# A second gated layer whose output is accumulated transposed in five of six token groups, with right-side tiles shifted by 96 bytes

## The chip, the cores and the metric

The kernel runs on one core of one Trainium2 chip. The metric is device time in microseconds (us) of the whole launch. An execution can be profiled: the profile has a start, an end and operands for the instructions of TensorE (PE, and PEld for its weight loads), VectorE (DVE), ScalarE (ACT), GpSimd (POOL) and SyncE (SP, which here only issues DMAs and waits).

## The reference, cut to what matters

A delta-rule attention over 4 batches of 768 tokens (8 heads of 48) gives rows of 384 numbers. Two dense layers follow, on 3,072 rows:

```python
h = np.maximum(x @ w_in, 0.0)            # 384 -> 2048
x = (h * h @ w_out)                      # 2048 -> 384
gate = 1.0 / (1.0 + np.exp(-(x @ w_gate)))   # 384 -> 1536
val = x @ w_val                              # 384 -> 1536
out = (gate * val @ w_out)                   # 1536 -> 384
```

The change lies in the last line, the product of `gate * val` (called p here) with the second `w_out`, 1536 by 384.

## The kernel before, in words

Tokens are cut into six groups of 512 (two chunks of 64 tokens of each of the four batches). In the first stage attention and the first layer run interleaved in an order written out by hand. The second stage (`moe2_h`, `moe2_o`, and the loop at L848) is the second layer alone, and the change is in it.

Every float32 operand is cut into a high and a low part of the type float32r, and each product is made in three passes: high by high, high by low, low by high. For each group g the layer's 1,536 inner features are cut into 12 blocks f of 128, so the stage has 72 steps n = 12g + f.

`moe2_h(n)` (L792) makes the gate and the val of one block: for each of the two, 3 passes by 3 blocks of 128 inputs, 9 matmuls at L802 with 512 moving columns (the tokens) and 128 by 128 stationary weights. Then ACT takes the sigmoid (L808), DVE multiplies (p, L810), ACT makes the high part `ph` (L812) and DVE the low part `pl` (L814).

`moe2_o(n)` (L819) adds the block's share to the output. Its stationary operand is `ph` or `pl` for one of four blocks m of 128 tokens, its moving operand the 384 columns of `w_out`: 12 matmuls at L832 a step, and each PSUM tile holds 128 tokens by 384 outputs. Three of its four PSUM tiles (o0 to o2) have a bank each, the fourth has one from another pool. After block 11 each tile is copied to SBUF by ACT (m = 0, 2; L841) or DVE (m = 1, 3; L839), and two DMAs each write 64 rows of 1,536 bytes (L845), eight a group.

The loop at L848 issues `moe2_h(n)` and then `moe2_o(n - 1)`, so TensorE always has a step of L802 between two steps of L832, and the last block's `moe2_o` of a group comes just after the first `moe2_h` of the next. At f = 2 SP loads the next group's input (L753, tile x2r); at f = 6, 7, 8 ACT and POOL split a third of it each (L758, helper lines L115 and L116). Each engine works through its own instructions in program order, and so does SP.

The weights of blocks f = 0 to 5 (`w2a`, L764) lie on the right side of SBUF, under the pool `w2x` (L763: staging for weights and input, and the sigmoid's tile). Those of f = 6 to 11 (`w2b`, L786) lie on the left, as do the tiles of x, `ph` and `pl`. A block's tile has 384 columns each of gate, val and output weights, once for the high part and once for the low.

Of the kernel before, what the change touches and what calls it, by code (L numbers as in the profile page):

```python
# [7 lines left out]
F32 = mybir.dt.float32  # L8
# [7 lines left out]
NB, NH, SEQ, HD = 4, 8, 768, 48  # L16
DM, FF1, FF2 = 384, 2048, 1536
C = 64
NSTEP = SEQ // C
NG = NSTEP // 2  # L20
# [63 lines left out]
def kernel(  # L84
# [637 lines left out]
    with tc.manual_schedule():  # L722
        for token in ORDER.split():
            run(token)
        w2_t, w2_new = {}, []

        def open_w2(fs, name, side):
            pool = ctx.enter_context(tc.tile_pool(name=name, bufs=1, side=side, reuse_waits="tile"))
            for f in fs:
                w2_t[f] = [pool.tile([128, 3 * DM], F32R, name=f"w2{h}{f}") for h in ("h", "l")]  # L730
                w2_new.append(f)

        w2_in = []

        def w2_load():
            if w2_new:
                f = w2_new.pop(0)
                t = w2x.tile([128, 3 * DM], F32, tag="t", name="t")
                nc.sync.dma_start(out=t, in_=w2d[:, f * 3 * DM:(f + 1) * 3 * DM])
                w2_in.append((f, t))  # L740

        def w2_split(n=1):
            while len(w2_in) > n:
                f, t = w2_in.pop(0)
                split(*w2_t[f], t, nc.vector)

        x2 = {}

        x2r = {}

        def load_x2(g):
            x2r[g] = w2x.tile([128, KD, GT], F32, tag="x2r", name="x2r")
            nc.sync.dma_start(out=x2r[g], in_=x2d[g])  # L753

        def split_x2(g, kc):
            if kc == 0:
                x2[g] = [work.tile([128, KD, GT], F32R, tag=f"x{h}", name=f"x{h}") for h in ("hi", "lo")]
            split(x2[g][0][:, kc], x2[g][1][:, kc], x2r[g][:, kc], nc.gpsimd)  # L758

        N1 = NG * NF1  # L760
        assert not (kt_t or kc_t or kn_t or v_t or q_t or pm_t or N_t or xr_t or yt_t or o_t)
        at.close()
        w2x = ctx.enter_context(tc.tile_pool(name="w2x", bufs=2, side="right"))  # L763
        open_w2(range(W2A), "w2a", "right")  # L764
        for n in range(N1 - NF1 + 2, N1 + 2):
            if n < N1:
                moe1_h(n)
            if n + 2 < N1:
                fetch_low(n + 2, 0)
            if n + 1 < N1:  # L770
                fetch_low(n + 1, 1)
            if n < N1:
                w2_split()
            moe1_o(n - 2)
            if n == N1 + 1:
                put_x2(NG - 1)
            if n < N1:
                if n % 2:
                    w2_load()
                moe1_g(n)  # L780
            if n == N1 - 7:
                load_x2(0)
            if N1 - 5 <= n < N1 - 2:
                split_x2(0, n - N1 + 5)
        p1.close()
        open_w2(range(W2A, NF2), "w2b", "left")  # L786

        obp = ctx.enter_context(tc.tile_pool(name="obp", bufs=4))
        ps_2 = ctx.enter_context(tc.tile_pool(name="ps_2", bufs=4, space=PSUM))
        p_t = {}  # L790

        def moe2_h(n):  # L792
            g, f = divmod(n, NF2)
            assert f not in w2_new and all(f != i for i, _ in w2_in)
            xh, xl = x2[g]
            pss = []
            for v in range(2):
                hi, lo = (w[:, v * DM:(v + 1) * DM] for w in w2_t[f])
                ps = ps_2.tile([128, GT], F32, tag="gv", name="gv")
                for i, (w, x) in enumerate([(hi, xh), (lo, xh), (hi, xl)]):  # L800
                    for kc in range(KD):
                        nc.tensor.matmul(  # L802
                            out=ps, lhsT=w[:, kc * 128:kc * 128 + 128], rhs=x[:, kc, :],
                            start=(i == 0 and kc == 0), stop=(i == 2 and kc == KD - 1),
                        )
                pss.append(ps)
            sg = w2x.tile([128, GT], F32, tag="sg", name="sg")
            nc.scalar.activation(out=sg, in_=pss[0], func=ACTF.Sigmoid)  # L808
            p = work.tile([128, GT], F32, tag="gg", name="p")
            nc.vector.tensor_tensor(out=p, in0=sg, in1=pss[1], op=ALU.mult)  # L810
            ph = work.tile([128, GT], F32R, tag="gh", name="ph", bufs=3)
            nc.scalar.copy(out=ph, in_=p)  # L812
            pl = work.tile([128, GT], F32R, tag="gl", name="pl", bufs=3)
            nc.vector.tensor_tensor(out=pl, in0=p, in1=ph.bitcast(F32), op=ALU.subtract)  # L814
            p_t[n] = (ph, pl)

        po2 = [None] * 4

        def moe2_o(n):  # L819
            g, f = divmod(n, NF2)  # L820
            if f == 0:
                po2[:] = [
                    ps_o.tile([128, DM], F32, tag=f"o{m}", name=f"o{m}") if m < 3
                    else ps_2.tile([128, DM], F32, tag="o3", name="o3", bufs=1)
                    for m in range(4)
                ]
            hi, lo = (w[:, 2 * DM:3 * DM] for w in w2_t[f])
            ph, pl = p_t.pop(n)
            for m in range(4):
                cs = slice(m * 128, m * 128 + 128)  # L830
                for i, (x, w) in enumerate([(ph, hi), (ph, lo), (pl, hi)]):
                    nc.tensor.matmul(  # L832
                        out=po2[m], lhsT=x[:, cs], rhs=w,
                        start=(f == 0 and i == 0), stop=(f == NF2 - 1 and i == 2),
                    )
                if f == NF2 - 1:
                    ob = obp.tile([128, DM], F32, tag="ob", name="ob")
                    if m % 2:
                        nc.vector.tensor_copy(out=ob, in_=po2[m])  # L839
                    else:  # L840
                        nc.scalar.copy(out=ob, in_=po2[m])  # L841
                    s = 2 * g + m // 2
                    for b in range(2):
                        r0 = (2 * (m % 2) + b) * SEQ + s * C
                        nc.sync.dma_start(out=out[r0:r0 + C, :], in_=ob[64 * b:64 * b + 64])  # L845

        N2 = NG * NF2
        for n in range(N2 + 1):  # L848
            if n < N2:
                moe2_h(n)  # L850
                w2_split(n < 2)
                g, f = divmod(n, NF2)
                if f == 2 and g + 1 < NG:
                    load_x2(g + 1)
                if 6 <= f < 9 and g + 1 < NG:
                    split_x2(g + 1, f - 6)
            w2_load()
            if n >= 1:
                moe2_o(n - 1)
# [5 lines left out]
def _layout(inputs):  # L865
    import numpy as np

    q, k, v, beta = (np.asarray(inputs[n]) for n in ("q", "k", "v", "beta"))

    def cut(a):  # L870
        return a.reshape((2, 2, 4, 2, NSTEP, C) + a.shape[3:])


    def places(x):
        x = cut(x)
        return np.stack([np.stack([x[:, a ^ c, :, a] for c in range(2)]) for a in range(2)])


    qc, kc, vc, bc = places(q), places(k), places(v), places(beta)

    def dims(x):
        return x.transpose(0, 6, 4, 1, 2, 3, 5).reshape(96, NSTEP, 16, C)

    def by_c(x):
        return x.transpose(1, 5, 4, 0, 2, 3, *range(6, x.ndim)).reshape((128, NSTEP, 16) + x.shape[6:])

    def by_a(x):
        return x.transpose(0, 5, 4, 1, 2, 3, 6).reshape(128, NSTEP, 16, HD)

    def lhs(w):  # L890
        return w.reshape(KD, 128, -1, 128).transpose(1, 2, 0, 3).reshape(128, -1, DM)

    def rhs(w):
        return w.reshape(-1, 128, DM).transpose(1, 0, 2)

    i = {n: np.ascontiguousarray(a).view(np.int64) for n, a in inputs.items() if n.startswith("moe")}
    arrays = {
        "kq": np.stack([dims(kc), dims(qc)], axis=2),
        "kn": by_c(kc),
        "vn": by_c(vc),  # L900
        "ks": by_a(kc),
        "beta": by_c(bc),
        "w1": np.concatenate([lhs(i["moe_w_in"]), rhs(i["moe_w_out"])], axis=2),
        "w2": np.concatenate(
            [lhs(i["moe2_w_gate"]), lhs(i["moe2_w_val"]), rhs(i["moe2_w_out"])], axis=2
        ).reshape(128, -1),
    }
    return {f"in_{n}_dram": np.ascontiguousarray(a) for n, a in arrays.items()}
# [20 lines left out]
```

## Time and profile before

| | us |
|---|---|
| time, median of 3 runs | 1146.42 |
| lowest and highest run | 1139.19, 1148.51 |
| the profiled execution's own time | 1144.12 |
| its span, first to last instruction | 1142.1 |
| TensorE busy in it | 1054.6 (92%) |

The span begins with the first instruction and ends with the last; 2.0 us of the profiled execution's time lie outside it. TensorE's matmuls are pipelined: each record of one is longer than the distance to the next one's start, so how fast TensorE goes is read from start to start, not from the durations.

### The profile page before, as it was taken

What the parts mean: (1) busy time and instruction counts of PE and PEld (TensorE: products, weight loads), DVE (VectorE), ACT (ScalarE), POOL (GpSimd) and SP (SyncE); (2) the same over time, 40 slices, a digit from 0 to 9 for tenths busy, and PEclk for the clock granted to TensorE, in tenths of its full rate; (3) what the DMA queues carried; (4) which work ended last, traced back from release to release, by engine and by line L of the source; (5) the groups of instructions that cost most, each with busy time, mean ns of one, the idle gap of its engine ahead of it and who ended that gap; (6) DMA issues with size and microseconds to landing.
All of it is one profiled execution on the core that took longest, in us unless ns stands there. A gap on an engine that the chain in (4) does not pass through costs nothing.

```text
span 1142.1 us, 27177 instructions
## 1 busy us (share of the span) xinstructions
PE 1054.6 (92%) x11890; PEld 893.0 (78%) x11890; DVE 580.6 (51%) x1102; ACT 430.7 (38%) x688; POOL 152.8 (13%) x118
## 2 busy tenths in 40 slices
PE   3485798899999989999999999999999999999997
PEld 2384676677887877788788888888888888888886
DVE  6638958896796887589253234322222222222222
ACT  2143355355455446445445563321222222222211
POOL 5223454211011011111110010100100001001000
PEclk9999878999999999899999999999999999999999
DMA  9327845495479457547645544010010020100101
GB/s 251 101 79 188 271 161 157 131 244 180 143 219 251 127 167 237 148 143 216 175 140 187 160 164 147 22 44 13 1 56 1 1 56 1 56 1 1 28 1 28
DMA packets 85223, 133.99 MB, mean 117 GB/s; under 512 B 33648, under 2 KB 66032, under 8 KB 85104
## 3 DMA queue, kind: packets, MB, share of 16 engines
q1 hardware_dynamic: 85104, 132.26, 39.5%
q8 instruction: 93, 1.52, 0.6%
q14 instruction: 26, 0.21, 0.1%
HBM read 104.69 MB, written 22.81 MB: 112 GB/s over the span
## 4 chain that ended last, share of the span: by engine, by line
PE 84%; DVE 6%; DMA 3%; SPq 2%; issue 2%; ACT 1%; POOL 1%; ACTq 0%; DVEq 0%; POOLq 0%
PE gv L802 26%; PE h L635 16%; PE o L672 16%; PE o L832 13%; PE att L351 2%; PE att L558 2%; PE att L340 1%; PE att L546 1%; PE att L500 1%; PE att L580 1%; PE att L515 1%; PE att L528 1%; DMA il<-w1d 1%; PE att L582 1%; DMA w1d<-wl 1%
## 5 line engine op out<-in xcount | busy, mean ns | idle before, releaser
L810 DVE TENSOR_TENSOR p<-sg,gv 128x512 f32<-128x512 f32 x72 | 49.5, 688 | 284.1 <-PE gv L802 284.1
L648 ACT ACTIVATE gg<-h 128x512 f32<-128x512 f32 x96 | 57.4, 598 | 191.1 <-PE h L635 171.1
L802 PE MATMUL gv<-xhi,w2l 128*128 128x512 f32 x432 | 123.3, 394 | 0.0
L802 PE MATMUL gv<-xhi,w2h 128*128 128x512 f32 x432 | 123.3, 394 | 0.0
L802 PE MATMUL gv<-xlo,w2h 128*128 128x512 f32 x432 | 123.2, 393 | 0.0
L672 PE MATMUL o<-gh,il 128*128 128x512 f32 x288 | 114.9, 399 | 0.0
L808 ACT ACTIVATE sg<-gv 128x512 f32<-128x512 f32 x72 | 43.1, 599 | 181.9 <-PE gv L802 181.9
L812 ACT CAST ph<-p 128x512 fp32r<-128x512 f32 x72 | 44.7, 620 | 159.2 <-DVE p L810 159.2
L832 PE MATMUL o<-w2h,pl 128*128 128x384 f32 x288 | 97.4, 338 | 0.0
L832 PE MATMUL o<-w2h,ph 128*128 128x384 f32 x288 | 97.2, 338 | 0.0
L832 PE MATMUL o<-w2l,ph 128*128 128x384 f32 x288 | 97.1, 337 | 0.0
L657 DVE TENSOR_TENSOR gl<-gg,gh 128x512 fp32r<-128x512 f32 x96 | 71.3, 744 | 50.6 <-ACT gg L651 50.4
L802 PEld LDWEIGHTS gv<-xlo,w2h 128*128 128x128 f32 x432 | 81.3, 188 | 18.9
L802 PEld LDWEIGHTS gv<-xhi,w2l 128*128 128x128 f32 x432 | 81.1, 188 | 18.8
L635 PE MATMUL h<-xhi,il 128*128 128x512 f32 x288 | 84.8, 404 | 9.0 <-DMA il<-w1d 9.0
L672 PE MATMUL o<-gl,w1h 128*128 128x512 f32 x216 | 86.4, 400 | 5.0 <-DVE gl L657 3.3
L802 PEld LDWEIGHTS gv<-xhi,w2h 128*128 128x128 f32 x432 | 80.3, 188 | 12.8
L672 PE MATMUL o<-gh,w1h 128*128 128x512 f32 x216 | 90.3, 418 | 0.0
L116 POOL TENSOR_TENSOR xlo<-x2r,xhi 128x512 fp32r<-128x512 f32 x18 | 24.6, 1368 | 398.8 <-ACT xhi L115 398.8
L814 DVE TENSOR_TENSOR pl<-p,ph 128x512 fp32r<-128x512 f32 x72 | 49.9, 693 | 49.4 <-ACT ph L812 49.4
L635 PEld LDWEIGHTS h<-xhi,il 128*128 128x128 f32 x288 | 56.3, 196 | 22.5 <-DMA il<-w1d 9.2
L635 PE MATMUL h<-xhi,w1h 128*128 128x512 f32 x216 | 67.6, 423 | 6.1 <-ACT xhi L115 6.1
(127 smaller groups left out, 1861.3 us busy)
## 6 DMA issues: line engine op xcount, KB each, us to landing
il<-w1d SPq DMA_DIRECT2D x192, 192.0 KB, 3.5
raw<-in_w_dram SPq DMA_DIRECT2D x25, 768.0 KB, 5.4
w1s<-in_w_dram SPq DMA_DIRECT2D x9, 768.0 KB, 5.8
w2d<-y SPq DMA_DIRECT2D x18, 384.0 KB, 5.6
t<-w2d SPq DMA_DIRECT2D x12, 576.0 KB, 4.1
w1d<-wl SPq DMA_DIRECT2D x16, 384.0 KB, 3.7
v<-in_vn_dram SPq DMA_DIRECT2D x12, 384.0 KB, 5.6
kn<-in_kn_dram SPq DMA_DIRECT2D x12, 384.0 KB, 5.0
```

What stands on the lines that cost most here:

```text
L116: eng.tensor_tensor(out=dst_lo, in0=src, in1=dst_hi.bitcast(F32), op=ALU.subtract)
L351: nc.tensor.matmul(out=psv[c][tok(a), k, :], lhsT=t[dim(a), 8 * c + k, :], rhs=q[dim(a), 8 * c + k, :], start=True, stop=True,)
L635: nc.tensor.matmul(out=ps[:, cs], lhsT=w[:, kc * 128:kc * 128 + 128], rhs=x[:, kc, cs], start=(i == 0 and kc == 0), stop=(i == 2 and kc == ...
L648: nc.scalar.activation(out=gg, in_=ps, func=ACTF.Relu)
L657: nc.vector.tensor_tensor(out=gl, in0=gg, in1=gh.bitcast(F32), op=ALU.subtract)
L672: nc.tensor.matmul(out=po[m], lhsT=w[:, cs], rhs=x, start=(f == 0 and i == 0), stop=(f == NF1 - 1 and i == 2),)
L802: nc.tensor.matmul(out=ps, lhsT=w[:, kc * 128:kc * 128 + 128], rhs=x[:, kc, :], start=(i == 0 and kc == 0), stop=(i == 2 and kc == KD - 1),)
L808: nc.scalar.activation(out=sg, in_=pss[0], func=ACTF.Sigmoid)
L810: nc.vector.tensor_tensor(out=p, in0=sg, in1=pss[1], op=ALU.mult)
L812: nc.scalar.copy(out=ph, in_=p)
L814: nc.vector.tensor_tensor(out=pl, in0=p, in1=ph.bitcast(F32), op=ALU.subtract)
L832: nc.tensor.matmul(out=po2[m], lhsT=x[:, cs], rhs=w, start=(f == 0 and i == 0), stop=(f == NF2 - 1 and i == 2),)
```

## The change

It does three things.

1. In groups 0 to 4 `moe2_o` hands over to a new function `moe2_ot`. The operands change places: the stationary one is a 128 by 128 block of `w_out`, the moving one `ph` or `pl` with all 512 tokens. There are three PSUM tiles of 128 outputs by 512 tokens, and 9 matmuls a step. After block 11 DVE turns each PSUM tile in blocks of 32 by 32 into one SBUF tile `ob` (128 by 16 by 96), by three `transpose` instructions. SP then issues 32 DMAs, each from 32 partitions, in runs of 96 numbers (384 bytes).
2. Group 5 keeps the old form. Since the columns of `w_out` are reordered on the host (`turned`) to suit the new form, its four copies out of PSUM write their 384 columns in runs of 32.
3. A tile of 24 float32 (96 bytes a partition) is put first into `w2x`, which shifts the right-side tiles of the second stage, `w2x`'s own and `w2a`, to multiples of 128 bytes.

```diff
         w2x = ctx.enter_context(tc.tile_pool(name="w2x", bufs=2, side="right"))
+
+        w2x.tile([128, 24], F32, name="pad", bufs=1)
...
+        obt = ctx.enter_context(tc.tile_pool(name="obt", bufs=2))
...
+        def moe2_ot(n):
+
+            g, f = divmod(n, NF2)
+            if f == 0:
+                po2[:KD] = [ps_o.tile([128, GT], F32, tag=f"o{m}", name=f"o{m}") for m in range(KD)]
+            hi, lo = (w[:, 2 * DM:3 * DM] for w in w2_t[f])
+            ph, pl = p_t.pop(n)
+            for m in range(KD):
+                for i, (w, x) in enumerate([(hi, ph), (lo, ph), (hi, pl)]):
+                    nc.tensor.matmul(
+                        out=po2[m], lhsT=w[:, m * 128:m * 128 + 128], rhs=x,
+                        start=(f == 0 and i == 0), stop=(f == NF2 - 1 and i == 2),
+                    )
+            if f == NF2 - 1:
+
+                ob = obt.tile([128, 16, KD * 32], F32, tag="obt", name="obt")
+                for m in range(KD):
+                    nc.vector.transpose(
+                        out=ob[:, :, 32 * m:32 * m + 32], in_=po2[m].rearrange("p (t i) -> p t i", i=32)
+                    )
+                for s in range(2):
+                    for b in range(NB):
+                        r0 = b * SEQ + (2 * g + s) * C
+                        for q in range(4):
+                            nc.sync.dma_start(
+                                out=out[r0:r0 + C, 96 * q:96 * q + 96].rearrange("(h i) d -> i h d", h=2),
+                                in_=ob[quad(q), 8 * s + 2 * b:8 * s + 2 * b + 2],
+                            )
+
         def moe2_o(n):
             g, f = divmod(n, NF2)
+            if g < NG - 1:
+                moe2_ot(n)
+                return
...
+                    o_out = ob.rearrange("p (q m i) -> p m q i", q=4, m=KD)
+                    o_in = po2[m].rearrange("p (m q i) -> p m q i", q=4, m=KD)
                     if m % 2:
-                        nc.vector.tensor_copy(out=ob, in_=po2[m])
+                        nc.vector.tensor_copy(out=o_out, in_=o_in)
                     else:
-                        nc.scalar.copy(out=ob, in_=po2[m])
+                        nc.scalar.copy(out=o_out, in_=o_in)
...
+    def turned(w):
+        return w.reshape(-1, 4, KD, 32).transpose(0, 2, 1, 3).reshape(w.shape)
...
-            [lhs(i["moe2_w_gate"]), lhs(i["moe2_w_val"]), rhs(i["moe2_w_out"])], axis=2
+            [lhs(i["moe2_w_gate"]), lhs(i["moe2_w_val"]), rhs(turned(i["moe2_w_out"]))], axis=2
```

## Rows read from the trace of the kernel before

**Rows 1.** The page, busy us and share of span by engine, instructions.
```profile
PE 1054.6 (92%) x11890; PEld 893.0 (78%) x11890; DVE 580.6 (51%) x1102; ACT 430.7 (38%) x688; POOL 152.8 (13%) x118
```

**Rows 2.** Stretches: length, busy us by engine, granted clock, DMA share, GB/s.
```profile
761.00:1131.00 370.00, 370.00 (x1770) 323.94 (x1769) 86.13 (x128) 82.03 (x140) 15.55 (x12) 1.00 0.07 20
```

**Rows 3.** Groups by form: count, busy us, mean ns, idle before.
```profile
L802 PE MATMUL gv<-xhi,w2h 128*128 128x512 f32 x432 | 123.3, 394 | 0.0
```

**Rows 4.** Timeline of TensorE, last left-side step (f = 11): start, length, what.
```profile
750.44 0.86 PE L802 MATMUL gv<-xhi,w2h 128*128 128x512 f32 x3
...
752.52 0.84 PE L802 MATMUL gv<-xhi,w2h 128*128 128x512 f32 x3
...
754.56 0.33 PE L832 MATMUL o<-w2h,ph 128*128 128x384 f32 x1
...
755.63 0.33 PE L832 MATMUL o<-w2h,ph 128*128 128x384 f32 x1
```

**Rows 5.** Timeline of TensorE, group 1: first right-side step, then first left-side step.
```profile
756.67 0.86 PE L802 MATMUL gv<-xhi,w2h 128*128 128x512 f32 x3
...
758.77 0.87 PE L802 MATMUL gv<-xhi,w2h 128*128 128x512 f32 x3
...
760.88 0.33 PE L832 MATMUL o<-w2h,ph 128*128 128x384 f32 x1
...
794.63 0.86 PE L802 MATMUL gv<-xhi,w2h 128*128 128x512 f32 x3
```

**Rows 6.** Timeline of TensorE, first L802 of group 2 and of group 5.
```profile
832.00 0.39 PE L802 MATMUL gv<-xhi,w2h 128*128 128x512 f32 x1
...
1058.01 0.62 PE L802 MATMUL gv<-xhi,w2h 128*128 128x512 f32 x2
```

**Rows 7.** Timeline of TensorE, first layer, a step of L672 and the next L635.
```profile
640.60 0.39 PE L672 MATMUL o<-gh,w1h 128*128 128x512 f32 x1
...
642.64 0.84 PE L635 MATMUL h<-xhi,w1h 128*128 128x512 f32 x3
```

**Rows 8.** Groups by form on DVE: two transposes, one copy from PSUM.
```profile
L437 DVE STREAM_TRANSPOSE t<-tt 128x1024 f32<-128x1024 f32 x6 | 14.0, 2326 | 0.1
...
L440 DVE STREAM_TRANSPOSE xi<-tt 128x1024 f32<-128x1024 f32 x6 | 12.1, 2011 | 0.0
...
L686 DVE COPY o<-o 128x512 f32<-128x512 f32 x6 | 4.1, 689 | 8.7 <-PE o L672 8.7
```

**Rows 9.** Timeline of DVE at the end of group 0.
```profile
761.15 0.69 DVE L810 TENSOR_TENSOR p<-sg,gv 128x512 f32<-128x512 f32 x1 [4.25 <-PE gv L802]
762.53 0.69 DVE L814 TENSOR_TENSOR pl<-p,ph 128x512 fp32r<-128x512 f32 x1 [0.69 <-ACT ph L812]
763.14 1.01 DVE L839 COPY ob<-o 128x384 f32<-128x384 f32 x2
767.47 0.69 DVE L810 TENSOR_TENSOR p<-sg,gv 128x512 f32<-128x512 f32 x1 [3.32 <-PE gv L802]
```

**Rows 10.** Timeline of SP, its DMA issues: end of group 0, end of the kernel.
```profile
762.90 5.04 SPq L845 DMA_DIRECT2D out_dram<-ob  x8
768.03 0.54 SPq L753 DMA_DIRECT2D x2r<-x2d  x1
...
1134.61 4.97 SPq L845 DMA_DIRECT2D out_dram<-ob  x8
```

**Rows 11.** Issues by line: count, KB each, median us to landing; then SP's time for one.
```profile
x2r<-x2d SPq DMA_DIRECT2D x6, 768.0 KB, 4.7
...
L284 SPq DMA_DIRECT2D k<-in_ks_dram x12: 391/433/6635, 18.1 to 551.9; - x12
L845 SPq DMA_DIRECT2D out_dram<-ob x48: 466/587/1256, 762.9 to 1139.0; - x48
```

**Rows 12.** Timeline of ACT at f = 6 of group 1.
```profile
800.27 0.62 ACT L115 CAST xhi<-x2r 128x512 fp32r<-128x512 f32 x1
803.21 0.60 ACT L808 ACTIVATE sg<-gv 128x512 f32<-128x512 f32 x1 [2.33 <-PE gv L802]
```

## The prediction

> **What bounds the kernel now.** I read the page's busy line first: TensorE is busy 92% of the span, DVE 51%, ACT 38% [rows 1]. Shares over the whole span hide stages, so I took the stretches next: over most of the second stage TensorE is busy all 370 of 370 us at granted clock 1.00, the upper level of 2.4 GHz, while DVE works 86 us of it, ACT 82 and the DMA engines have a share of 0.07 [rows 2]. The reader is to see that nothing feeds TensorE too late there. So only two things can move the time: how long TensorE itself takes for a step, and a new wait.
>
> A matmul's record lasts 394 ns [rows 3], but the next starts much earlier, so the cost of one is the distance between starts in the timeline. Three such distances carry the argument.
>
> In the first layer's last group, where stationary blocks and moving columns have the shape that the new form will have, nine matmuls of L672 take 642.64 - 640.60 = 2.04 us, or 226.7 ns each [rows 7]. 512 columns at 2.4 GHz are 213.3 ns, so 13.3 ns are a fixed cost of one matmul.
>
> In a left-side step of the second layer (f = 11), L802's second nine take 754.56 - 752.52 = 2.04 us, again 226.7 each, but the first nine take 2.08. L832's first six take 1.07 and, up to the next step's start at 756.67, its last six 1.04, which is 173.3 each: 160 for 384 columns and the same 13.3 [rows 4, 5]. So there is a slow spell after each switch of width: 0.04 us after 384 gives way to 512, 0.03 after the reverse. The first layer never changes width between these two lines, and I find none there.
>
> In a right-side step the slow spell doesn't end: L802 takes 2.10 and 2.11 for its halves, 4.21 against 4.12 on the left [rows 4, 5].
>
> **The change part by part.**
>
> *Fewer, wider matmuls.* 12 x 384 and 9 x 512 are both 4,608 columns; three fixed costs of 13.3 ns go: 2.08 - 2.04 = 0.04 us a step. Five groups have 60 steps: **2.4 us**. The Trainium skill's page "TensorE: Matmul & The Clock Gate" (section "Wait — 56ns, not 53.3ns?") puts the fixed part at about 2.5 ns, by which these 60 steps would give 0.45 us and the whole sum 8 us. The trace's 13.3 decides for me.
>
> *One width instead of two.* With 512 columns in both lines nothing switches in groups 0 to 4, and 0.07 us a step would go: **4.2 us**. It is bounded by 0 (the spell has another cause) and 4.2; I take the upper end, because the first layer alternates two lines of equal width at 226.7 without a spell.
>
> *The 96 bytes.* If the right side's slowness is its addresses, L802 gains 4.21 - 4.12 = 0.09 us in the 36 steps with f < 6: **3.2 us**, 0.5 of it in group 5. The bounds are 0 and 3.2. I take the upper end, because left-side tiles of the same shape, read by the same instruction, don't show it; the place rather than the offset could also make it, and no row separates them.
>
> These overlap in the right-side steps, so the sum is made once more from whole groups. The first L802 of groups 2 and 5 lie 1058.01 - 832.00 = 226.01 us apart, 75.34 a group [rows 6]. The new group is 12 steps of 27 matmuls at 226.7 ns, 12 x 6.12 = 73.44. That is 1.90 a group, 9.5 in five, and 0.5 in group 5 by its right-side steps: **10.0 us**, against 9.8 from the parts.
>
> *Turning the output on DVE.* No row turns 128 x 512 out of PSUM. Below stands the copy of that size from PSUM, 0.69 us; above, a whole 128 x 1024 transpose with both sides strided, 2.33 [rows 8]. I take half of the 2.01 of the transpose whose input is contiguous, as here: 1.0 us, so 3.0 a group, where two copies took 1.01 on DVE [rows 9]. In order they stand behind pl, which ends 763.22 - 760.88 = 2.34 us after L832's last block begins; they end at 5.3. Behind them waits the next p, which came 6.59 after [rows 9] and will come at about 6.4. TensorE needs the three banks again from 6.12 on, the last of them 6 x 226.7 ns later, at 7.48. The cover holds up to (7.48 - 2.34) / 3 = 1.71 us a transpose. Cost taken: 0; at 2.33 the last bank is 1.85 us late, five times, 9 us.
>
> *32 DMAs for 8 on SP.* Eight issues took 5.04 us, some 0.62 each with what lies between [rows 10]; 32 take 19.8. Each needs all three transposes, so they run from 5.3 to 25.1 after the block's begin. Behind them is the next group's input load, 4.7 us to landing [rows 11]: there at 29.9. ACT reads it at 800.27 - 760.88 = 39.4 [rows 12], 38.2 with six faster steps. Cost 0, with 8.3 us to spare. On the DMA engines the same bytes go out in a stretch where they are at 0.07 [rows 2]; `obt` has two buffers, so a late landing is waited for only two groups on.
>
> *Less on ACT, the last group's copies.* Two ACT copies a group go, off the path. In group 5 the copies write in runs of 32. The end is SP's eight issues, 1134.61 to 1139.58 [rows 10], so only the first copy's length counts: between 0 and about its own 0.5 us again (1.01 for two on DVE [rows 9]); I take 0, as the count per partition is the same. Extra SBUF and the reordered weights cost no instruction.
>
> **The sum** is 1144.1 - 10.0 = 1134.1 us for the profiled execution. That one lay 2.3 under the median of the runs, so against the median: 1146.4 - 10.0 = **1136.4**.
>
> **Rivals.**
>
> *The 96 bytes do nothing* (0.20). Right-side steps then keep 4.21, and their new L832, whose stationary operand now is the right-side tile, takes 9 x 234 = 2.11 against 6.327 - 4.21 = 2.12; 6.327 is (794.63 - 756.67) / 6 [rows 5]. They gain 0.01. Left-side steps go from (832.00 - 794.63) / 6 = 6.228 [rows 5, 6] to 6.12: 30 x 0.108 and 30 x 0.01 make 3.5, **1142.9**. The page "SBUF — State Buffer" of the Trainium skill (section "Specifications (TRN2)") has lines of 16 bytes, of which 96 are six whole ones, so by it this is the case. Against it stands that one instruction has two speeds by side.
>
> *The spell stays* (0.18): it comes from what L802 reads, not from the switch. 10.0 - 4.2 = 5.8, **1140.6**. For it: the new stage differs from the first layer in what DVE reads from PSUM meanwhile. Against: L802 begins at 762.99, its first nine are the slow ones, and from pl's end until the next p at 767.47 DVE does only the group's copies [rows 9].
>
> *The transposes are late* (0.05): above 1.71 us each; at 2.33 the 9 us eat the gain, **1145.6**.
>
> *SP is late, and the kernel slower* (0.05). If a 32-partition issue costs double, 1.24, 32 take 39.7 and the load lands 11.6 us after ACT wants it. ACT's next sigmoid stands behind that split. It comes 2.9 us after it [rows 12], and its chain (sigmoid, p, ph, some 2 us) feeds the L832 that begins two steps of 6.12 after the one during which the split starts, some 10.5 us behind it, so about 8 us more pass before TensorE waits. Then 3.6 to 4 us are lost, five times, some 19: **1155**. It decides from 0.62 + (8.3 + 8) / 32 = 1.13 us an issue on. Against: loading 384 KB in runs of 192 bytes was issued in 0.43, so many short runs don't make an issue long [rows 11].
>
> **How the numbers follow.** My forecast has 0.52. About 1% is what a measurement can tell from no change here; that bound is 1135.0, just under the forecast, and the runs shown spread by 9 us, so of the forecast's 0.52 nearly half falls under it with the measurement. All other cases lie within 1%, but for the worse half of SP's. Faster 0.26, same 0.71, slower 0.03. The range goes from 1131.5 (forecast less twice the 2.3 us between profile and median) to 1145 (the first rival and 2.3).
>
> **What would show it.** Right: TensorE's starts 226.7 apart throughout groups 0 to 4 on both sides of SBUF, a group 73.4 us, no idle before L802 or the new matmuls; three transposes of about 1.0 us after pl; 32 issues in about 20 us; group 5's left-side steps as before, its right-side ones like them. Wrong: 234 still at f < 6 (the offset), 2.08 still in L802's first nine (the width), a wait of TensorE for a transpose at a group's begin, or ACT waiting for x2r at f = 6.

## The result, and the profile after

The changed kernel takes **1134.86 us** (median of 8 runs, 1132.14 to 1140.18) against 1144.74 for the kernel before in 8 runs; the ratio is **0.9907**, 95% interval 0.9881 to 0.9932. That is 9.9 us less; 10.0 were forecast. The forecast's 1136.4 counted its 10.0 from a median of three runs, 1146.42; counted from the median of eight it is 1134.7.

The profiled execution took 1137.47, with a span of 1135.8. In its page the second stage's lines are L805 (gate and val, L802 before), L831 (the new form) and L867 (the old form, kept in group 5). The stretch from the second stage's begin to group 5:

```profile
687.30:1058.00 370.70, 370.70 (x1637) 307.07 (x1636) 100.94 (x141) 90.97 (x146) 20.01 (x15) 1.00 0.11 31
```

TensorE is still busy all the time at granted clock 1.00, as before [rows 2]; what changed is its pace. The timeline of TensorE in the changed kernel (start, length, what), with the left-side step f = 11 of group 0, the first right-side step of group 1, the first L805 of group 2, and the first step of group 5 in which L805 is followed by the old form (L867):

```profile
758.61 0.84 PE L805 MATMUL gv<-xhi,w2h 128*128 128x512 f32 x3
...
760.65 0.84 PE L805 MATMUL gv<-xhi,w2h 128*128 128x512 f32 x3
...
762.69 0.39 PE L831 MATMUL o<-ph,w2h 128*128 128x512 f32 x1
...
764.73 0.84 PE L805 MATMUL gv<-xhi,w2h 128*128 128x512 f32 x3
...
766.77 0.84 PE L805 MATMUL gv<-xhi,w2h 128*128 128x512 f32 x3
...
768.81 0.39 PE L831 MATMUL o<-ph,w2h 128*128 128x512 f32 x1
...
838.17 0.61 PE L805 MATMUL gv<-xhi,w2h 128*128 128x512 f32 x2
...
1064.67 0.86 PE L805 MATMUL gv<-xhi,w2h 128*128 128x512 f32 x3
...
1066.75 0.84 PE L805 MATMUL gv<-xhi,w2h 128*128 128x512 f32 x3
...
1068.79 0.33 PE L867 MATMUL o<-w2h,ph 128*128 128x384 f32 x1
```

Every nine matmuls take 2.04 us, in both halves of L805, in L831, on the left (758.61 to 764.73) and on the right (764.73 to 768.81); before it was 2.08 in one half on the left and 2.10 and 2.11 on the right [rows 4, 5]. A group takes 838.17 - 764.73 = 73.44 us against 75.34 [rows 6]. In group 5, where the widths still switch, the first half is 1066.75 - 1064.67 = 2.08 again.

The two ends of the second stage (its first L802 or L805, and its last matmul), kernel before and then changed kernel:

```profile
683.45 0.39 PE L802 MATMUL gv<-xhi,w2h 128*128 128x512 f32 x1
...
1135.29 0.34 PE L832 MATMUL o<-w2h,pl 128*128 128x384 f32 x1
```

```profile
687.21 0.39 PE L805 MATMUL gv<-xhi,w2h 128*128 128x512 f32 x1
...
1128.89 0.34 PE L867 MATMUL o<-w2h,pl 128*128 128x384 f32 x1
```

The stage is 451.84 us long before and 441.68 after: **10.2 less**. The two spans differ by only 6.3, since in this execution the first stage, which the change doesn't touch, ended 3.8 later. Over the twelve profiled executions in which that stage's matmuls run at their pace of before (all below but one) the second stage begins between 682.96 and 687.21. So below I compare the second stage's own length, first L805 to last matmul, which such differences don't enter.

What came with the new form, at the end of group 0: the group of transposes, then DVE's timeline and SP's.

```profile
L839 DVE STREAM_TRANSPOSE obt<-o 128x512 f32<-128x512 f32 x15 | 9.5, 686 | 0.0
```

```profile
764.33 0.69 DVE L817 TENSOR_TENSOR pl<-p,ph 128x512 fp32r<-128x512 f32 x1 [0.69 <-ACT ph L815]
764.94 1.91 DVE L839 STREAM_TRANSPOSE obt<-o 128x512 f32<-128x512 f32 x3
769.08 0.69 DVE L813 TENSOR_TENSOR p<-sg,gv 128x512 f32<-128x512 f32 x1 [2.23 <-PE gv L805]
```

```profile
766.87 14.93 SPq L846 DMA_DIRECT2D out_dram<-obt  x32
781.90 0.36 SPq L753 DMA_DIRECT2D x2r<-x2d  x1
```

A transpose takes 0.69 us, three end 4.2 us after the last block's matmuls began (762.69), and 2.2 us of idle DVE are left before the next p [rows 8, 9]. SP's 32 issues take 14.93 us here, 0.47 each, and 15.6 to 16.4 in the four later groups (0.49 to 0.51), against 0.62 for the old ones [rows 10]; the next input's load is issued 19 us before ACT first reads it, at 800.92.

### The profile page after: what moved, and what is told of

Same layout as the page of the kernel before. It is cut to its first block, busy times and chain, and to the rows that moved or that the text cites. A ratio compares the mean times of both kernels' runs of the same rounds, so it can differ in the third digit from the quotient of the medians.

```text
span 1135.8 us, 26916 instructions
## 1 busy us (share of the span) xinstructions
PE 1048.7 (92%) x11710; PEld 870.3 (77%) x11710; DVE 584.1 (51%) x1107; ACT 427.3 (38%) x678; POOL 153.4 (14%) x118
## 4 chain that ended last, share of the span: by engine, by line
PE 85%; DVE 7%; issue 2%; DMA 2%; ACT 1%; SPq 1%; POOL 0%; ACTq 0%; DVEq 0%; POOLq 0%
PE gv L805 26%; PE h L635 17%; PE o L672 16%; PE o L831 11%; PE o L867 2%; PE att L351 2%; PE att L558 2%; PE att L340 1%; PE att L546 1%; PE att L500 1%; PE att L580 1%; PE att L515 1%; PE att L528 1%; PE att L582 1%; DMA il<-w1d 1%
## 5 line engine op out<-in xcount | busy, mean ns | idle before, releaser
L805 PE MATMUL gv<-xhi,w2h 128*128 128x512 f32 x432 | 121.5, 389 | 0.0
L805 PE MATMUL gv<-xlo,w2h 128*128 128x512 f32 x432 | 121.4, 389 | 0.0
L805 PE MATMUL gv<-xhi,w2l 128*128 128x512 f32 x432 | 121.4, 389 | 0.0
L672 PE MATMUL o<-gh,il 128*128 128x512 f32 x288 | 114.5, 397 | 0.0
L635 PE MATMUL h<-xhi,il 128*128 128x512 f32 x288 | 86.3, 410 | 9.5 <-DMA il<-w1d 9.4
L805 PEld LDWEIGHTS gv<-xhi,w2l 128*128 128x128 f32 x432 | 81.1, 188 | 17.0
L805 PEld LDWEIGHTS gv<-xlo,w2h 128*128 128x128 f32 x432 | 81.1, 188 | 17.0
L805 PEld LDWEIGHTS gv<-xhi,w2h 128*128 128x128 f32 x432 | 81.0, 188 | 16.2
L672 PE MATMUL o<-gh,w1h 128*128 128x512 f32 x216 | 90.5, 419 | 0.0
L672 PE MATMUL o<-gl,w1h 128*128 128x512 f32 x216 | 86.6, 401 | 2.3 <-DVE gl L657 2.3
L635 PEld LDWEIGHTS h<-xhi,il 128*128 128x128 f32 x288 | 57.1, 199 | 23.6 <-DMA il<-w1d 9.6
L158 POOL TENSOR_TENSOR y<-raw 128x768 f32<-128x768 f32 x18 | 28.5, 1582 | 337.9 <-DVE raw L151 299.1
L635 PE MATMUL h<-xhi,w1h 128*128 128x512 f32 x216 | 68.3, 427 | 5.6 <-ACT xhi L115 5.6
L831 PE MATMUL o<-ph,w2h 128*128 128x512 f32 x180 | 70.0, 389 | 0.0
L831 PE MATMUL o<-ph,w2l 128*128 128x512 f32 x180 | 70.0, 389 | 0.0
```

The lines of the kernel that those rows point to most:

```text
L158: nc.gpsimd.tensor_tensor(out=t, in0=c["t"], in1=c["raw"][:, :, 0].bitcast(F32), op=ALU.add)
L635: nc.tensor.matmul(out=ps[:, cs], lhsT=w[:, kc * 128:kc * 128 + 128], rhs=x[:, kc, cs], start=(i == 0 and kc == 0), stop=(i == 2 and kc == ...
L672: nc.tensor.matmul(out=po[m], lhsT=w[:, cs], rhs=x, start=(f == 0 and i == 0), stop=(f == NF1 - 1 and i == 2),)
L805: nc.tensor.matmul(out=ps, lhsT=w[:, kc * 128:kc * 128 + 128], rhs=x[:, kc, :], start=(i == 0 and kc == 0), stop=(i == 2 and kc == KD - 1),)
L831: nc.tensor.matmul(out=po2[m], lhsT=w[:, m * 128:m * 128 + 128], rhs=x, start=(f == 0 and i == 0), stop=(f == NF2 - 1 and i == 2),)
```

## Experiments

Line numbers in the rows shift by the length of an edit. L805 and L831 stand for the two lines throughout.

### One part at a time: the pad alone, and all but the pad

```diff
 # kernel before
+        w2x.tile([128, 24], F32, name="pad", bufs=1)
```

> The kernel before with the 96-byte pad and nothing else. Theory (the offset of the right-side tiles costs): the steps with f < 6 become like those with f >= 6, L802 4.12 us instead of 4.21 and L832 2.106 instead of 2.119; a group takes 12 x 6.227 = 74.7 us instead of 75.34, and the whole 36 x (0.09 + 0.013) = 3.7 us less, a ratio of 0.997. Rival (the right side itself is slow, whatever the offset): L802 at f < 6 stays 4.21, a group 75.34, ratio 1.000.

```diff
 # changed kernel
-        w2x.tile([128, 24], F32, name="pad", bufs=1)
```

> The changed kernel without the pad. Theory (offset): L805 at f < 6 goes back to 4.21 us, and the new L831, whose stationary operand is now a right-side tile, to 9 x 234 = 2.11 at f < 6; at f >= 6 both stay 4.08 and 2.04, so that a group takes 6 x 6.32 + 6 x 6.12 = 74.6 us instead of 73.44. Ratio to the kernel before 0.997. Rival (equal width alone lets TensorE keep its pace, and the offset hurt only where widths switch): 73.44 a group, as with the pad, ratio 0.991.

Measured in the same session: the pad alone 0.9956 of the kernel before (interval 0.994 to 0.9973), all but the pad 0.9949 (0.9931 to 0.9967). TensorE in the kernel with the pad alone, first right-side step of group 1 and the begin of group 2:

```profile
755.88 0.86 PE L803 MATMUL gv<-xhi,w2h 128*128 128x512 f32 x3
...
757.96 0.84 PE L803 MATMUL gv<-xhi,w2h 128*128 128x512 f32 x3
...
760.00 0.33 PE L833 MATMUL o<-w2h,ph 128*128 128x384 f32 x1
...
830.60 0.63 PE L803 MATMUL gv<-xhi,w2h 128*128 128x512 f32 x2
```

The right-side step is now a left-side one: halves of 2.08 and 2.04, 4.12 in all, 74.72 us a group. The stage is 448.09 long, 3.75 less than before, where 3.7 was expected.

The same view without the pad: the second right-side step of group 1, then a left-side step:

```profile
762.58 0.86 PE L804 MATMUL gv<-xhi,w2h 128*128 128x512 f32 x3
...
766.79 0.39 PE L830 MATMUL o<-ph,w2h 128*128 128x512 f32 x1
...
806.58 0.84 PE L804 MATMUL gv<-xhi,w2h 128*128 128x512 f32 x3
...
810.66 0.39 PE L830 MATMUL o<-ph,w2h 128*128 128x512 f32 x1
```

On the right 4.21, on the left 4.08; 74.73 us a group (756.33 to 831.06), 448.84 the stage, 3.0 less than before (3.5 expected). Both rivals (slow by place; slow only where widths switch) fall. The two parts give 3.75 and 3.0 alone and 10.2 together, because in a right-side step neither part alone gets its full share: such a step falls from 6.33 to 6.23 with the pad, to 6.32 with the new form, and to 6.12 with both. With the pad alone the switch of width still costs 0.07. With the new form alone L804 stays at 4.21, since its offset slows it with or without a switch, and L830 takes 2.11 (766.79 to 768.90) where L832 took 2.12: its stationary operand is now a right-side tile, so it too pays for the offset, and that eats what the fewer matmuls and the equal width give. The ratios' centres lie 1.3 and 2.8 us lower than the trace's 3.75 and 3.0 make them; 0.997 lies in the first interval and just outside the second. The stage lengths are what I rely on.

### Is it the offset or the side, and how far off?

```diff
 # changed kernel, in open_w2
+            if side == "left":
+                pool.tile([128, 8], F32, name="shift")
             for f in fs:
```

> The changed kernel with a tile of 32 bytes a partition put first among the left-side weights, so that the blocks f = 6 to 11 lie 32 bytes past where they lay, while the right side stays on multiples of 128 bytes. Theory (offset): now the left-side steps are the slow ones, L805 4.21 us and L831 2.11 at f >= 6, and those at f < 6 stay 4.08 and 2.04; a group 74.6 us. Rival (place): all steps stay 6.12, a group 73.44.

```diff
 # changed kernel
-        w2x.tile([128, 24], F32, name="pad", bufs=1)
+        w2x.tile([128, 8], F32, name="pad", bufs=1)
```

> The changed kernel with a pad of 32 bytes in place of 96, so that the right-side tiles lie 64 bytes off a multiple of 128. First theory (only multiples of 128 are fast): L805 at f < 6 4.21 us, a group 74.6 to 74.7, as without the pad. Second (64 is enough): 4.08 and 73.44.

```diff
 # changed kernel
-        w2x.tile([128, 24], F32, name="pad", bufs=1)
+        w2x.tile([128, 28], F32, name="pad", bufs=1)
```

> The changed kernel with a pad of 112 bytes, so that the right-side tiles lie 16 bytes off a multiple of 128. If the cost is the same whatever the offset: L805 at f < 6 4.21 us, a group 74.6 to 74.7. If it grows with the offset: half as much as at 32 bytes or less, a group under 74.1. If 16 bytes are enough: 73.44.

TensorE with the left side shifted by 32 bytes: a right-side step (f = 2), then a left-side one (f = 8) up to the next:

```profile
770.07 0.84 PE L807 MATMUL gv<-xhi,w2h 128*128 128x512 f32 x3
...
774.15 0.39 PE L833 MATMUL o<-ph,w2h 128*128 128x512 f32 x1
...
807.10 0.86 PE L807 MATMUL gv<-xhi,w2h 128*128 128x512 f32 x3
...
811.30 0.40 PE L833 MATMUL o<-ph,w2h 128*128 128x512 f32 x1
...
813.40 0.40 PE L807 MATMUL gv<-xhi,w2h 128*128 128x512 f32 x1
```

Now the left is slow, 4.20 and 2.10, and the right keeps 4.08: the slowness goes with the offset and not with the side. A group takes 74.58.

The same step (f = 2, right side) at 64 bytes off, then at 16:

```profile
772.07 0.86 PE L805 MATMUL gv<-xhi,w2h 128*128 128x512 f32 x3
...
776.27 0.39 PE L831 MATMUL o<-ph,w2h 128*128 128x512 f32 x1
```

```profile
768.26 0.87 PE L805 MATMUL gv<-xhi,w2h 128*128 128x512 f32 x3
...
772.47 0.40 PE L831 MATMUL o<-ph,w2h 128*128 128x512 f32 x1
```

4.20 both times, and 74.57 us a group both times. So 16, 32 and 64 bytes off cost the same to within a nanosecond: 2.10 / 9 = 233 ns a matmul (234 without the pad, 32 off on the right) instead of 226.7. Neither does 64 suffice, nor does the cost grow with the offset. The three kernels ran once each (1141.60, 1143.25 and 1139.49 us); their second stages took 447.72, 447.73 and 447.72, 6.0 more than the changed kernel's.

### Does the moving operand count too?

```diff
 # changed kernel: work (x, ph, pl, gh, gl) 32 bytes on, the weights back on 128
+    work.tile([128, 8], F32, name="shift", bufs=1)
...
+    w1p.tile([128, 24], F32, name="back1")
...
+            if side == "left":
+                pool.tile([128, 24], F32, name="back2")
```

> The changed kernel with the working tiles (x, ph, pl, and in the first stage gh, gl) 32 bytes past where they were, and the left-side weights back on their old place by a second tile of 96 bytes, in both stages. So the moving operands are off a multiple of 128 bytes and the stationary ones are on it. First theory (only the stationary operand's offset counts): L805 4.08 and L831 2.04 us as in the changed kernel, a group 73.44, and the first layer's nine matmuls 2.04. Second (any operand read off the multiple is slow): L805 about 4.21 and L831 2.11 at every f, a group 75.8, and the first layer's nine about 2.11.

One time, 1152.98 us, slower than the kernel before. TensorE, a step of the second stage (f = 2, right side, on its multiple of 128):

```profile
776.60 0.86 PE L809 MATMUL gv<-xhi,w2h 128*128 128x512 f32 x3
...
780.80 0.39 PE L835 MATMUL o<-ph,w2h 128*128 128x512 f32 x1
...
782.90 0.40 PE L809 MATMUL gv<-xhi,w2h 128*128 128x512 f32 x1
```

4.20 and 2.10, although the weights lie well; 75.71 us a group. The first layer's nine matmuls, 2.04 before [rows 7], took 2.10 to 2.11 as well (one of L635's steps ran from 660.88 to 662.98), and the second stage began 3 to 7 us later than in the other runs. The theory that the stationary operand alone counts falls: either operand off a multiple of 128 bytes makes the 512-column matmul slow.

With 384 columns the runs don't show that cost. In group 5 of this run the old form's stationary operand, `ph` or `pl`, lies 32 bytes off:

```profile
1089.88 0.34 PE L871 MATMUL o<-w2h,ph 128*128 128x384 f32 x1
...
1091.98 0.85 PE L809 MATMUL gv<-xhi,w2h 128*128 128x512 f32 x3
```

Its twelve matmuls take 2.10 us, where those of group 5 in the changed kernel take 2.11. With the moving operand 32 bytes off, twelve take 2.12 on the right side of the kernel before and 2.08 on the left with the shift there.

### Is the slow spell the switch of width?

```diff
 # changed kernel, moe2_ot
+                    k = GT if f in (0, NF2 - 1) else DM
                     nc.tensor.matmul(
-                        out=po2[m], lhsT=w[:, m * 128:m * 128 + 128], rhs=x,
+                        out=po2[m][:, 0:k], lhsT=w[:, m * 128:m * 128 + 128], rhs=x[:, 0:k],
```

> The changed kernel with only 384 of the 512 token columns in L831's matmuls of the blocks f = 1 to 10 (the last 128 columns of their share are left out of the output). Operands, places and engines are as in the changed kernel; only the width switches again between L805 and L831. Theory (the slow spell comes from the switch of width): L805's first nine go from 2.04 back to 2.08 us and L831 takes 9 x 173.3 = 1.56 plus about 0.03. Rival (the spell came from the old operand order or from what L802 reads): L805 stays 2.04 in both halves and L831 takes 1.56.

```diff
 # the same, and in moe2_h
+                        k = DM if g < NG - 1 and 0 < f < NF2 - 1 else GT
                         nc.tensor.matmul(
-                            out=ps, lhsT=w[:, kc * 128:kc * 128 + 128], rhs=x[:, kc, :],
+                            out=ps[:, 0:k], lhsT=w[:, kc * 128:kc * 128 + 128], rhs=x[:, kc, 0:k],
 # ... and [:, 0:k] in sigmoid, p, ph and pl
```

> As the narrow run before, but L805's matmuls too have only 384 columns in the blocks f = 1 to 10 of groups 0 to 4, and sigmoid, p, ph and pl with them (the last 128 columns of these blocks' share are left out of the output). Theory (the slow spell comes from the switch between two widths): with 384 in both lines there is no spell; inside f = 2 to 10 L805 takes 18 x 173.3 = 3.12 us with two equal halves of 1.56, and L831 9 x 173.3 = 1.56. Rival (384 columns are too short to hide a weight load of 188 ns, the loads fall behind and the next matmuls pay for it, whatever their width): L805's halves are longer than 1.56, up to 9 x 188 = 1.69, and L831 longer than 1.56.

The two kernels, each of which leaves out a part of the work, ran once each (1113.19 and 1063.27 us). TensorE, step f = 6 of group 1, first with 512 in L805 and 384 in L831:

```profile
785.87 0.86 PE L805 MATMUL gv<-xhi,w2h 128*128 128x512 f32 x3
...
787.95 0.84 PE L805 MATMUL gv<-xhi,w2h 128*128 128x512 f32 x3
...
789.99 0.33 PE L832 MATMUL o<-ph,w2h 128*128 128x384 f32 x1
...
791.58 0.63 PE L805 MATMUL gv<-xhi,w2h 128*128 128x512 f32 x2
```

then with 384 in both:

```profile
771.31 0.68 PE L806 MATMUL gv<-xhi,w2h 128*128 128x384 f32 x3
...
772.87 0.68 PE L806 MATMUL gv<-xhi,w2h 128*128 128x384 f32 x3
...
774.43 0.33 PE L833 MATMUL o<-ph,w2h 128*128 128x384 f32 x1
...
775.99 0.51 PE L806 MATMUL gv<-xhi,w2h 128*128 128x384 f32 x2
```

With two widths the spell is back in the new form: 2.08, then 2.04, and 1.59 for L831 where nine at 173.3 are 1.56. With one width it is gone although the width is 384: 1.56, 1.56, 1.56. So neither the old operand order nor what L805 reads makes it, nor a weight load of 188 ns that 384 columns couldn't hide. It is the switch: 0.04 us into the wider, 0.03 into the narrower.

### The cover: transposes three times over, output DMAs four times as many

```diff
 # changed kernel
-                for m in range(KD):
+                for m in (0, 0, 0, 1, 1, 1, 2, 2, 2):
                     nc.vector.transpose(
```

> The changed kernel with each transpose made three times, nine a group at 0.69 us each. Theory (the cover is as reckoned: DVE starts them 2.34 us after the last block's matmuls begin, TensorE wants the last bank 7.48 after): the last bank comes free at 2.34 + 6.2 = 8.5, TensorE waits 1.1 us at the third bank's first matmul of each of the groups 1 to 5, 5.3 us in all, and p of the next step waits too, without a further loss. Rival (the PSUM banks are not what is waited for first: DVE's late p stops TensorE as well): more than 8 us in all. Rival (covered still): 0.

One time, 1140.64; the stage 449.08, **7.4 more** than the changed kernel's. DVE and TensorE at the first such place (the last block's matmuls had begun at 758.44):

```profile
760.70 6.41 DVE L839 STREAM_TRANSPOSE obt<-o 128x512 f32<-128x512 f32 x9
```

```profile
765.70 0.39 PE L831 MATMUL o<-pl,w2h 128*128 128x512 f32 x1
767.25 0.47 PE L831 MATMUL o<-ph,w2h 128*128 128x512 f32 x1 [1.17 <-DVE obt L839]
```

The wait is where it was reckoned, at the third bank's first matmul, once in each of groups 1 to 5. Only its size was short: the ninth transpose ends at 767.11, TensorE starts 0.14 later, so from start to start 1.55 us pass in place of 0.23; with some 0.1 in the matmuls behind it that is 1.4 a group, 1.7 before group 5. The late p stopped nothing more.

```diff
 # changed kernel
-                            nc.sync.dma_start(
-                                out=out[r0:r0 + C, 96 * q:96 * q + 96].rearrange("(h i) d -> i h d", h=2),
-                                in_=ob[quad(q), 8 * s + 2 * b:8 * s + 2 * b + 2],
-                            )
+                            for h in range(2):
+                                for j in range(2):
+                                    nc.sync.dma_start(
+                                        out=out[r0 + 32 * h:r0 + 32 * h + 32, 96 * q + 48 * j:96 * q + 48 * j + 48],
+                                        in_=ob[quad(q), 8 * s + 2 * b + h, 48 * j:48 * j + 48],
+                                    )
```

> The changed kernel with each output DMA cut into four (32 partitions by 48 numbers), 128 a group instead of 32, the same bytes. Theory (SP works in order, and the load of the next input behind the issues is what gets late): at 0.35 to 0.47 us an issue they end 49 to 64 us after the block begins, the load lands 4.4 later, 15 to 31 us after ACT wants it, and some 8 of that pass before TensorE waits; the loads of groups 2 to 5 stand behind such issues, so four times 7 to 23 us, 28 to 90 us in all, and the first thing to wait is ACT's split of x2r. Rival (output DMAs are off every path): 0, a group 73.44.

One time, 1235.09; the stage 543.26, 101.6 more. Its waits (who for whom: us in total, times, longest), then SP and ACT in group 1, then a stretch as in [rows 2]:

```profile
ACT xhi L115 <- DMA x2r<-x2d: 123.9, 4, 31.4
...
PE o L831 <- ACT ph L815: 90.9, 4, 23.1
```

```profile
762.35 60.69 SPq L848 DMA_DIRECT2D out_dram<-obt  x128
```

```profile
828.23 0.62 ACT L115 CAST xhi<-x2r 128x512 fp32r<-128x512 f32 x1 [31.13 <-DMA x2r<-x2d]
```

```profile
827.00:834.00 7.00, 3.23 (x8) 2.51 (x9) 2.76 (x4) 3.89 (x7) 2.86 (x3) 0.50 0.03 10
```

The chain is the one described: 128 issues of 0.47 us hold back the load behind them, ACT stands 31 us at its split, everything behind that split on ACT stands with it, and after 8 us of it TensorE waits too, 22.7 on average, four times. The rest, some 2.7 us each time, is mostly a slow restart: the first nine matmuls of L831 after the wait took 4.0 us instead of 2.04 (830.77 to 834.77), and the granted clock around them is 0.50, the lower level of 1.2 GHz; TensorE had stood idle for 22.9 us before them. At that level six starts from 831.36 to 833.92 lie 427 ns apart, which is 512 columns at 1.2 GHz with nothing added.

### The last DMAs issued from two engines

```diff
 # changed kernel, group 5
-                        nc.sync.dma_start(out=out[r0:r0 + C, :], in_=ob[64 * b:64 * b + 64])
+                        (nc.scalar if m == 2 or m == 3 and b else nc.sync).dma_start(out=out[r0:r0 + C, :], in_=ob[64 * b:64 * b + 64])
```

> The changed kernel with the last group's (group 5's) eight output DMAs shared between two issuing engines: SP keeps those of m = 0 and 1 and one of m = 3, ACT issues those of m = 2 and the other of m = 3. Theory (the end is set by SP's eight issues of 0.62 us one after the other): SP issues five, 3.1 us instead of 5.04, and the time falls by about 1.9 us, a ratio to the kernel before of 0.9895 against 0.991 for the changed kernel; the last issue then follows DVE's last copy. Rival (the landing of the last DMAs, not their issue, sets the end): under 0.5 us less.

Median 1132.92 us of 5 runs, ratio to the kernel before **0.9895** (0.9878 to 0.9913). SP's issues at its end (ACT's three take 1.84 us, from 1128.63 on):

```profile
1127.59 3.17 SPq L882 DMA_DIRECT2D out_dram<-ob  x5
```

SP's queue is 3.17 us long as expected, and from the last matmul to the end it is 5.5 us instead of 6.9: 1.4 gained, not 1.9, as the end now comes 3.0 us after SP's last issue instead of 2.5. The intervals of this version and of the changed kernel overlap, so by their times the two are not told apart; the trace's tail tells them apart. The second stage, which this edit leaves alone up to its last matmul, took 441.68 us again.

## Why the prediction was right

**Fewer, wider matmuls (2.4 us).** The fixed cost of 13.3 ns a matmul is the same at both widths once nothing else hinders: 173.3 at 384 and 226.7 at 512, each held over whole steps at granted clock 1.00. It isn't fixed at every clock: at 0.50 the starts were 427 ns apart, 512 columns and no more. The Trainium skill's 2.5 ns ("TensorE: Matmul & The Clock Gate", "Wait — 56ns, not 53.3ns?") doesn't fit these float32r passes.

**One width (4.2 us).** The upper bound was right, and its reason too: the spell is the switch. But on the right side it came only together with the pad: without it the new form gave 3.0 us, where this term and the one above make 6.6.

**The 96 bytes (3.2 us).** The upper bound again, and a little more: alone the pad gave 3.75, as the mean right-side step fell by 0.10 and not 0.09, L832's 0.01 among it. The rival that the addresses do nothing fell in four runs: the slowness left the right with the pad, stayed without it, moved to the left with a shift there, and came at 16 bytes too. The Trainium skill gives SBUF lines of 16 bytes ("SBUF — State Buffer", "Specifications (TRN2)"). They don't describe what TensorE pays here: a shift by one whole line, 16 bytes, cost as much as one by 64.

**The sum.** A group was forecast at 73.44 us and took 73.44; the stage fell by 10.2 where 10.0 was said.

**Turning on DVE (0).** Right that it is covered. A transpose took 0.69, the lower end of my range and not the 1.0 taken: out of PSUM into runs of 32 it costs what a copy of that size does [rows 8], two thirds of the time per column of the transposes in SBUF. Three transposes left 2.2 us before p. The bound of 1.71 us each was of the right kind: three times the work, 2.1 a bank, did make TensorE wait.

**SP (0).** Right in the effect, wrong in the size: 0.47 to 0.51 us an issue, not 0.62. In group 0 the load went out 6 us earlier than reckoned, 5 of them by the issues and 1 by the shorter transposes. The mechanism of the rival is real, as the run with 128 DMAs shows, but I counted five late loads where only four stand behind outputs of an earlier group.

**Group 5's copies (0).** L867's two tiles on DVE took 0.56 us each, as before (L839's last two took 0.56 each), and SP's eight issues 5.04 against 4.97 [rows 10].

What stays open: why a switch of width, or an operand off a multiple of 128 bytes, makes TensorE lose some nanoseconds a matmul. The runs show when, not why. Nor do they show that 128 is the whole rule: no trace lists addresses, and within one side of SBUF the second stage's operands start multiples of 512 bytes apart. That the fast places are multiples of 128 comes from the layout of the tiles. Measured is that 16, 32 and 64 bytes off is slow; a shift by a whole 128 was made only for the left-side weights of the run with the shifted working tiles, where the moving operand was slow anyway.

## What to carry to other kernels

When TensorE is busy all the time and still short of its pace, look at the distances between starts, per line and per operand's place, and compare them with a stretch of the same kernel that runs at the best pace; the difference times the count is the gain, and here it was the whole gain. Where matmuls have 512 float32r columns, as here, lay out both operands' tiles on multiples of 128 bytes, and give neighbouring lines of matmuls the same width. One such hindrance can keep the removal of another from paying, so an edit that gains little alone may be worth keeping for the next.

## What the runs showed that I had not expected

- The offset costs the same, 233 ns instead of 226.7 a matmul of 512 columns, at 16, 32 and 64 bytes, and in either operand; lines of 384 columns next to them don't show it.
- Of two back-to-back lines of matmuls the switch of width costs 0.03 to 0.04 us spread over the next six to nine matmuls; two lines of 384 columns run without it.
- A 32 by 32 transpose of 128 x 512 from PSUM on DVE takes 0.69 us; of 128 x 1024 in SBUF 2.0 to 2.3.
- A DMA of 24 KB in 64 runs of 384 bytes takes SP 0.47 to 0.51 us to issue, one of 96 KB in 64 runs of 1,536 bytes 0.62.
